# Moving the first loads of x and of the weights into one DMA queue, two weight chunks to a load, and dropping a touch load, at the head of a gated attention and FFN kernel

## The chip, the cores and the metric

The kernel runs on one core of a Trainium2 chip. The metric is the device time of one execution in microseconds (us). The kernel before takes 274.06 us (median of three runs, 273.92 to 274.57). A run counts as slow when it is over 1.5% above the fastest of the same kernel, and as fast otherwise; all runs that are compared here are fast unless the text says otherwise. In every profiled run the device time is 1.25 to 1.34 us longer than the span of the profile (for example 273.55 us against a span of 272.2 us).

Times of events are us from the start of the profile's span. "Landing" of a load means the last of its completion events in the DMA records of the trace.

## The reference, cut to what matters

```python
x = A_x                                            # (1, 2048, 640) bf16
g = sigmoid((x * gate_w).sum(-1))
q, k, v = split(x @ wqkv)                          # wqkv (640, 1920): columns q, k, v
a = linear_attention(phi(q), phi(k), v) @ wo       # phi(t) = (t + 1 or exp(t)) + 1e-6
b = (gelu(x @ w_gate) * (x @ w_up)) @ w_down
out = g * a + (1 - g) * b
```

The kernel computes the k and q projections first, for 16 tiles of 128 rows of x. Only this start matters here. It needs the first two tiles of x (x0, x1), the five 128-row chunks of the k columns of wqkv (wk0 to wk4) and the five of the q columns (wq0 to wq4). Each of these twelve blocks is 128 rows of 1280 bytes, 160 KB.

## The kernel before: the parts that the change and the argument touch

Loads are issued by SyncE ("sp") and by ScalarE ("act"); each has a DMA queue of its own. A load increments a semaphore, and its consumers wait for that.

```python
P.op("act", lambda e: e.dma_start(touch[0:16, 0:4], A_wqkv[0:128:8, 640:644]),   # 16 pieces of 8 B
     writes=[P.res("touch")], dma=new_dma_key())
load_x(0)
load_wk(0)
load_x(1, "act")
load_wk(1)
load_wk(3)
# ... a dummy Exp on ScalarE, so that its table is loaded early
load_wk(2, "act")
load_wk(4, "act")
P.op("dve", lambda e: e.memset(gw_sb, 0.0), writes=[r_gw])
dma_in(gw_sb[0:5, :], gate_w.rearrange("(k p) -> k p", p=128), [r_gw], eng="act")
for k in range(KC):                                # KC = 5
    load_wq(k, ("sp", "act")[k % 2])
# tiles 2..15 of x come transposed by DMA; the first of them waits for wk4
for i in range(NXN, NT):
    load_xT(i, after=([r_wk[4]] if i == NXN else ()))
```

TensorE's program at the head. `warm(n, w)` is n throw-away matmuls of w columns, which keep TensorE busy while it waits. `T` transposes a tile of x on TensorE, and VectorE copies the result back to SBUF. `KM(n, [k])` and `QM(n, [k])` are the projection of tile n by weight chunk k, each one matmul of 512 columns and one of 128 or 129.

```python
warm(5, 512)
warm(1, 128)
T(0, [0], 7)
T(0, [1, 2, 3, 4], 6)
warm(6, 128)
KM(0, [0])                  # needs wk0
T(1, [0], 7)                # needs x1
T(1, [1, 2, 3, 4], 6)
warm(3, 128)
KM(1, [0])
for k in (1, 2, 3):
    KM(0, [k])              # needs wk k
    KM(1, [k])
gate_col()                  # needs the gate weights
# ... chunk 4, then the ten QM of both tiles with the exp and max work between
for i in range(2, NT):
    KQ(i)                   # the tile loop: k and q projection of the other 14 tiles
```

## Time and profile before

| What | Value | Where it stands |
|---|---|---|
| device time | 274.06 us, median of 3 | times |
| TensorE busy | 267.9 of 272.2 us (98%) | busy table of the page |
| first projection matmul | 4.38 us | timeline |
| second weight chunk starts (KM of chunk 1) | 5.46 us | timeline |
| tile loop starts | 10.39 us | timeline |

TensorE is nearly always busy, but part of that at the head is throw-away work. So the question for a change of the first loads is at what time the useful chain starts, not how busy an engine is.

The chain of waits of the kernel before, its first pieces; columns are start (us), length (us), what. "SPq" is SyncE issuing a DMA, "PE ps" a matmul, L451 the 512-column matmul of KM.

```profile
0.79 0.41 SPq L340
...
1.26 2.98 DMA pool<-in_A_wqkv_dram
...
4.38 0.38 PE ps L451
```

The load that starts at 1.26 us is wk0. It takes 2.98 us to land, and the first projection matmul starts right after it. From there the chain stays on TensorE until 10.30 us.

TensorE's timeline of the kernel before; columns are start, length, engine, line, operation, output and input, count, and in brackets the idle time before and what ended it. L417 is warm-up, L431 the transposes, L451 and L452 are KM, L536 is the tile loop.

```profile
3.02 0.74 PE L431 MATMUL ps<-pool 128*128 128x128 bf16 x5
3.55 0.62 PE L417 MATMUL ps<-const-bfloat16-1.0 128*128 128x128 bf16 x6
4.38 0.38 PE L451 MATMUL ps<-pool 128*128 128x512 bf16 x1 [0.21 <-DMA pool<-in_A_wqkv_dram]
...
4.64 0.44 PE L431 MATMUL ps<-pool 128*128 128x128 bf16 x5
...
5.46 0.38 PE L451 MATMUL ps<-pool 128*128 128x512 bf16 x1
...
10.39 1.24 PE L536 MATMUL ps<-pool 128*128 128x512 bf16 x5
```

Tile 0 meets wk0 at 4.38, tile 1 is transposed at 4.64 when x1 has come, chunk 1 starts at 5.46, the tile loop at 10.39.

The DMA view of the kernel before, over 0 to 8 us in slices of 0.2 us: GB/s moved in each slice.

```profile
GB/s 0 0 0 0 0 0 0 0 0 186 179 282 269 147 83 243 365 384 301 275 275 371 378 378 397 384 391 353 245 259 270 275 359 390 410 365 403 391 339 254
```

The first slice with traffic is 1.8 to 2.0 us. The rate dips at 2.6 to 3.0 us (147 and 83 GB/s), is back at 365 at 3.2, and stays mostly above 270.

### The profile page before, as it was taken

To read this page: it belongs to the slowest core of one execution; us is meant where nothing else is said; L and a number is where in the kernel's file an instruction comes from. 1 tells how busy PE (TensorE), PEld (TensorE's weight loads), DVE (VectorE), ACT (ScalarE), POOL (GpSimd) and SP (SyncE) were. 2 spreads that over 40 slices of the span, in tenths; PEclk is the share of its full clock that TensorE was granted. 3 is DMA by queue.
4 is the path that set the end of the run, shared out by engine and by line. 5 is a ranking of instruction groups with operands and counts; after the bars stand their busy time and mean duration, and the time that the engine had idled before them with its cause. 6 is when DMAs were issued, how large, how long until landed. Compare 5 with 4: busy or idle time off the path is not lost.

```text
span 272.2 us, 3426 instructions
## 1 busy us (share of the span) xinstructions
PE 267.9 (98%) x1343; PEld 128.1 (47%) x1369; DVE 141.8 (52%) x251; ACT 75.9 (28%) x132; POOL 30.0 (11%) x28
## 2 busy tenths in 40 slices
PE   8999999999999999999999999999999999999997
PEld 4555555544445444444444444444444444444444
DVE  2689898997333335999999999634110000000200
ACT  2555555210422453332222232224011122121021
POOL 5000000003140002242332421000000000000000
PEclk9999999999999999999999999999999999999999
DMA  6776999500300011612221221272031110110211
GB/s 219 176 114 124 349 402 384 119 2 19 61 16 2 23 50 51 200 28 48 27 48 30 43 50 25 60 229 96 5 79 37 41 39 19 39 41 19 58 58 41
DMA packets 42208, 23.61 MB, mean 87 GB/s; under 512 B 31567, under 2 KB 40783, under 8 KB 42063
## 3 DMA queue, kind: packets, MB, share of 16 engines
q1 hardware_dynamic: 41429, 22.56, 30.5%
q10 hardware_dynamic: 762, 0.82, 0.8%
q8 instruction: 11, 0.18, 0.3%
q14 instruction: 6, 0.05, 0.1%
HBM read 13.83 MB, written 2.63 MB: 60 GB/s over the span
## 4 chain that ended last, share of the span: by engine, by line
PE 95%; DVE 2%; DMA 1%; issue 1%; ACT 1%; SPq 0%; DVEq 0%; ACTq 0%
PE ps L697 41%; PE ps L861 23%; PE ps L536 12%; PE ps L593 6%; PE ps L840 4%; PE ps L808 2%; PE ps L675 2%; PE ps L596 2%; DMA pool<-in_A_wqkv_dram 1%; PE ps L451 1%; PE ps L821 1%; PE ps L466 1%; DVE pool L490 1%; PE ps L718 1%; DVE pool L555 1%
## 5 line engine op out<-in xcount | busy, mean ns | idle before, releaser
L697 PE MATMUL ps<-pool 128*128 128x512 bf16 x510 | 113.0, 379 | 0.5
L697 PEld LDWEIGHTS ps<-pool 128*128 128x128 bf16 x520 | 50.4, 98 | 60.1
L861 PE MATMUL ps<-pool 128*128 128x512 bf16 (+2 forms) x300 | 62.4, 367 | 0.3
L703 ACT ACTIVATE pool<-ps 128x512 f32<-128x512 f32 x52 | 31.0, 597 | 73.1 <-PE ps L697 73.1
L705 DVE TENSOR_TENSOR pool<-ps,pool 128x512 bf16<-128x512 f32 x52 | 34.6, 689 | 31.7 <-PE ps L697 30.4
L861 PEld LDWEIGHTS ps<-pool 128*128 128x128 bf16 x306 | 29.1, 98 | 33.5 <-issue 0.4
L536 PE MATMUL ps<-pool 128*128 128x512 bf16 (+1 forms) x206 | 37.9, 344 | 0.2
L844 DVE TENSOR_TENSOR pool<-ps,pool 128x512 bf16<-128x512 f32 x4 | 2.8, 692 | 61.5 <-PE ps L840 61.5
L751 POOL TENSOR_TENSOR pool<-pool 128x640 f32<-128x640 bf16 x16 | 22.5, 1406 | 72.8 <-DVE pool L753 65.9
L868 ACT ACTIVATE pool<-ps,pool 128x512 bf16<-128x512 f32 (+1 forms) x16 | 10.9, 680 | 68.6 <-PE ps L861 68.6
L536 PEld LDWEIGHTS ps<-pool 128*128 128x128 bf16 x210 | 20.5, 98 | 17.5
L555 DVE SCALAR_TENSOR_TENSOR pool<-ps,pool 128x128 bf16<-128x128 f32 (+2 forms) x42 | 25.3, 603 | 2.4
L546 ACT ACTIVATE pool<-ps 128x640 bf16<-128x640 f32 x28 | 19.7, 703 | 18.1 <-DVE pool L555 10.6
L593 PE MATMUL ps<-pool 128*128 128x512 bf16 x76 | 19.2, 380 | 0.1
L761 DVE TENSOR_TENSOR pool<-pool 128x640 bf16<-128x640 bf16 x16 | 13.2, 825 | 0.6
L759 DVE TENSOR_SCALAR pool<-pool 128x32 f32<-128x32 f32 x16 | 12.8, 803 | 0.6
L753 DVE TENSOR_REDUCE pool<-pool 128x32 f32<-128x640 f32 x16 | 12.9, 809 | 0.0
L641 DVE TENSOR_TENSOR pool<-pool 128x640 f32<-128x640 f32 x14 | 11.6, 826 | 0.5
L840 PE MATMUL ps<-pool 128*128 128x512 bf16 x51 | 11.5, 380 | 0.1
L643 POOL PARTITION_ALL_REDUCE pool<-pool x1 | 4.0, 3971 | 60.7 <-DVE pool L641 60.7
L593 PEld LDWEIGHTS ps<-pool 128*128 128x128 bf16 x78 | 6.9, 98 | 7.2
L552 DVE TENSOR_SCALAR pool<-pool 128x640 bf16<-128x640 bf16 x28 | 9.1, 327 | 1.8 <-ACT pool L546 0.4
(70 smaller groups left out, 105.0 us busy)
## 6 DMA issues: line engine op xcount, KB each, us to landing
out_dram<-pool SPq DMA_DIRECT2D x19, 128.0 KB, 1.7
pool<-in_B_w_gate_dram SPq DMA_DIRECT2D x1, 2080.0 KB, 14.2
pool<-in_B_w_up_dram SPq DMA_DIRECT2D x1, 2080.0 KB, 18.8
pool<-in_A_x_dram SPq DMA_DIRECT2D x1, 1280.0 KB, 8.7
pool<-in_B_w_down_dram SPq DMA_DIRECT2D x1, 1120.0 KB, 6.1
pool<-omg_row SPq DMA_DIRECT2D x1, 1024.0 KB, 4.8
pool<-in_A_wqkv_dram SPq DMA_DIRECT2D x6, 160.0 KB, 4.4
pool<-in_A_x_dram SPq DMA_DIRECT2D x1, 960.0 KB, 5.8
```

Of the source, the lines that this page charges most:

```text
L536: last = e.matmul(ps[:, b + p, 0:c1 - c0], xT[:, k, i * 128:(i + 1) * 128], wkq[:, k, c0:c1], start=(k == 0), stop=(k == KC - 1))
L546: P.op("act", lambda e: e.activation(e_buf[m], ps_flat[:, o:o + 640], ACT.Exp), reads=banks, writes=[r_e[m]])
L555: P.op("dve", lambda e, c0=c0, c1=c1: e.scalar_tensor_tensor(dst[:, c0:c1], ps_flat[:, o + c0:o + c1], 1.0 + EPS, e_buf[m][:, c0:c1], ALU. ...
L593: last = e.matmul(ps[:, b, :], pk[i][:, c * 128:(c + 1) * 128], x_aug[:, i, 0:512], start=(i == 0), stop=(i == NT - 1))
L697: last = e.matmul(ps[:, b, :], w[:, k, fc * 128:(fc + 1) * 128], xT[:, k, j * 512:(j + 1) * 512], start=(k == 0), stop=(k == KC - 1))
L703: P.op("act", lambda e: e.activation(ge[n], ps[:, gb, :], ACT.Gelu_apprx_tanh), reads=[bank[gb]], writes=[r_ge[n]])
L705: P.op("dve", lambda e: e.tensor_tensor(hT[fc][:, j * 512:(j + 1) * 512], ps[:, ub, :], ge[n], ALU.mult), reads=[bank[ub], r_ge[n]], write ...
L751: P.op("pool", lambda e: e.tensor_tensor(tmp[n], pq[i], z_b, ALU.mult), reads=[r_pq[i], r_zb], writes=[r_tmp[n]])
L753: P.op("dve", lambda e: e.tensor_reduce(den[n], tmp[n].rearrange("p (h d) -> p h d", h=32), AX.X, ALU.add), reads=[r_tmp[n]], writes=[r_de ...
L761: P.op("dve", lambda e: e.tensor_tensor(pq[i].rearrange("p (h d) -> p h d", h=32), pq[i].rearrange("p (h d) -> p h d", h=32), den[n].unsqu ...
L840: last = e.matmul(ps[:, b, :], wd[:, fc, 512:640], hT[fc][:, j * 512:(j + 1) * 512], start=False, stop=(fc == NFC - 2), skip_group_check=True)
L861: last = e.matmul(ps[:, pb, 0:c1 - c0], lhs, rhs, start=False, stop=(q == len(rows) - 1), skip_group_check=True)
```

## The change

The intent is to give wk0, which gates the first projection, the DMA engines to itself: everything goes into SyncE's queue in the order of use, so nothing from a second queue runs beside wk0. The weights come mostly two chunks to a load, to save issues. The touch load goes, the gate weights are loaded first on ScalarE. The wait for wk4 before the transposed loads goes as well, since those now stand behind the weights in the same queue. Five warm-ups go, as less waiting is expected.

```diff
-            P.op("act", lambda e: e.dma_start(touch[0:16, 0:4], A_wqkv[0:128:8, 640:644]),
-                 writes=[P.res("touch")], dma=new_dma_key())
+            P.op("dve", lambda e: e.memset(gw_sb, 0.0), writes=[r_gw])
+            dma_in(gw_sb[0:5, :], gate_w.rearrange("(k p) -> k p", p=128), [r_gw], eng="act")
             load_x(0)
-            load_wk(0)
-            load_x(1, "act")
-            load_wk(1)
-            load_wk(3)
+            load_w(wk, 640, 0, 1, r_wk)
+            load_x(1)
+            load_w(wk, 640, 1, 3, r_wk)
+            load_w(wk, 640, 3, 5, r_wk)
+            load_w(wq, 0, 0, 2, r_wq)
+            load_w(wq, 0, 2, 4, r_wq)
+            load_w(wq, 0, 4, 5, r_wq)
 ...
-            load_wk(2, "act")
-            load_wk(4, "act")
-            P.op("dve", lambda e: e.memset(gw_sb, 0.0), writes=[r_gw])
-            dma_in(gw_sb[0:5, :], gate_w.rearrange("(k p) -> k p", p=128), [r_gw], eng="act")
-            for k in range(KC):
-                load_wq(k, ("sp", "act")[k % 2])
 ...
-                load_xT(i, after=([r_wk[4]] if i == NXN else ()))
+                load_xT(i)
 ...
             T(0, [1, 2, 3, 4], 6)
-            warm(6, 128)
+            warm(2, 128)
             KM(0, [0])
 ...
-            warm(3, 128)
+            warm(2, 128)
             KM(1, [0])
```

More of the change, by code (lines that the diff above doesn't have):

```diff
@@ L219, in bass_gated_mix__linear_attn_block__geglu_ffn__prompt_kernel @@
     O_GW = take(128)
-    O_TOUCH = take(16)
     TOTAL = off
@@ L300, in bass_gated_mix__linear_attn_block__geglu_ffn__prompt_kernel @@
             gw_sb = v16(O_GW, 128)
-            touch = v16(O_TOUCH, 16)
             bank = [P.res("bank%d" % b, excl=True) for b in range(8)]
@@ L341, in dma_in @@
                      reads=reads, writes=writes, dma=new_dma_key())
-            def load_x(i, eng="sp"):
-                dma_in(x_aug[:, i, 0:640], A_x[0, i * 128:(i + 1) * 128, :], [r_xn[i]], eng=eng)
-            def load_wk(k, eng="sp"):
-                dma_in(wk[:, k, :], A_wqkv[k * 128:(k + 1) * 128, 640:1280], [r_wk[k]], eng=eng)
-            def load_wq(k, eng="sp"):
-                dma_in(wq[:, k, 0:640], A_wqkv[k * 128:(k + 1) * 128, 0:640], [r_wq[k]], eng=eng)
-            P.op("act", lambda e: e.dma_start(touch[0:16, 0:4], A_wqkv[0:128:8, 640:644]),
-                 writes=[P.res("touch")], dma=new_dma_key())
@@ L357, in bass_gated_mix__linear_attn_block__geglu_ffn__prompt_kernel, with load_x, load_w @@
-            load_x(0)
-            load_wk(0)
-            load_x(1, "act")
-            load_wk(1)
-            load_wk(3)
+            def load_x(i):
+                dma_in(x_aug[:, i, 0:640], A_x[0, i * 128:(i + 1) * 128, :], [r_xn[i]])
+            def load_w(dst, c0, k0, k1, res):
+                dma_in(dst[:, k0:k1, 0:640],
+                       A_wqkv[k0 * 128:k1 * 128, c0:c0 + 640].rearrange("(k p) w -> p k w", p=128), res[k0:k1])
+            P.op("dve", lambda e: e.memset(gw_sb, 0.0), writes=[r_gw])
@@ L366, in bass_gated_mix__linear_attn_block__geglu_ffn__prompt_kernel, with load_xT @@
-            load_wk(4, "act")
-            P.op("dve", lambda e: e.memset(gw_sb, 0.0), writes=[r_gw])
-            dma_in(gw_sb[0:5, :], gate_w.rearrange("(k p) -> k p", p=128), [r_gw], eng="act")
-            for k in range(KC):
-                load_wq(k, ("sp", "act")[k % 2])
-            def load_xT(i, after=()):
+            def load_xT(i):
                 P.op("sp", lambda e: e.dma_start_transpose(xT[:, :, i * 128:(i + 1) * 128],
                                                            A_x[0, i * 128:(i + 1) * 128, :]),
-                     reads=list(after), writes=[r_xT[i]], dma=new_dma_key())
+                     writes=[r_xT[i]], dma=new_dma_key())
```

## The prediction

> **What bounds the kernel now.** TensorE: busy 267.9 of 272.2 us (98%, busy table), 95% of the chain of waits, granted clock full from 3.77 us on. Only the head can gain. There TensorE runs throw-away warm-ups until x0 lands (timeline); the chain of waits is SyncE's issue of x0 (at 0.79 us), the load of wk 0 (issued 1.26, 2.98 us long), then matmuls without a break to 10.23. So wk 0 gates the first projection matmul (4.38 us). Landings, from the DMA records: x0 2.97, wk0 4.24, x1 4.42, wk1 5.41, wk2 5.60, wk3 6.25, wk4 6.50, wq0 7.40, wq1 7.84, wq2 8.26, wq3 8.93, wq4 8.97, first transposed x tile (xT2) 10.19; its matmuls start at 10.39. After 4.38 TensorE waits for DMA only 0.16 us more (wk1).
>
> **What the change does.**
> 1. wk0 no longer shares the 16 engines with x1 and wk1. The Trainium skill (DMA: Bandwidth & Descriptors, "Queues, rings and completion order") says that an engine alternates between its rings packet by packet; the trace agrees: packets of both queues run side by side from 3.0 to 8.4 us. In one queue, wk0 follows x0 directly. 160 KB at the 326 to 360 GB/s of 4 to 8 us (windows table) is 0.46 to 0.50 us; estimated landings: wk0 3.5, x1 4.0, wk1-2 5.0, wk3-4 5.95, wq0-1 6.95, wq2-3 7.9, wq4 8.4.
> 2. Two chunks to a load delay the first of each pair by about 0.48 us, but TensorE takes a chunk each 0.55 us (5.46, 6.01, 6.55 in the timeline), so pairs stay ahead if the rate holds. SyncE issues a load each 0.47 us: eight end at 4.5, not limiting.
> 3. Five fewer warm-ups of 128 columns (0.06 us each at full clock, 0.11 at half): they only filled waiting. If wk0 lands at 3.5, the first projection matmul starts near 3.65, partly at half clock.
> 4. Touch load gone, gate weights earlier: x0 unchanged within 0.1 us.
> 5. The transposed loads no longer wait for wk4 (SyncE waited 2.5 us): issued from about 4.6 instead of 6.51, but behind the weights in the same queue, so xT2 lands 9.4 to 10.1, again only just before its use.
>
> **How much is on the critical path.** First projection matmul 0.7 us earlier; then x1 (4.0) and wk1-2 (5.0) stretch the gaps, so the second chunk starts at about 5.05 instead of 5.46: 0.4 us. From there TensorE is continuous, and the tile loop starts at about 10.0 instead of 10.39. Everything later is bound by TensorE, so the shift survives to the end.
>
> **Predicted time:** 273.7 us (0.13% less), range 273.1 to 274.3. Chances: faster by over 2% 0.003, within 2% 0.994, slower by over 2% 0.003. Any gain at all: about 85%.
>
> **What would show it.** wk0 landing at 3.4 to 3.7; first 128x512 projection matmul before 3.9; a short TensorE wait for wk1-2; tile loop starting at 9.9 to 10.2; later stages unchanged.
>
> **What would make it wrong.** A single queue that can't fill the engines (wk1-2 after 5.4); a slow first DMA without the touch load; the transposes taking engine time from wq; xT2 later than 10.2. The clock: the skill (TensorE: Matmul & The Clock Gate, "The HAM clock gate") says that activity over a window of about 3.4 us sets it; here it rose 2.95 us after the first warm-up, and fewer warm-ups with waits between could delay it, at up to about 0.5 us.

## The result, and the profile after

The changed kernel takes 274.06 us (median of six runs, 273.89 to 275.58), the kernel before 274.04 us in the same rounds (six runs, 273.85 to 274.57). The ratio is 1.0008, with a 95% interval of 0.9985 to 1.0032. A ratio here is the mean time of one kernel's fast runs over that of the other's of the same rounds, so not quite the ratio of the medians quoted. The time is the same; the forecast gain of 0.36 us isn't there.

The chain of waits of the changed kernel, its first pieces (L443 is now the 512-column matmul of KM):

```profile
0.79 0.40 SPq L338
...
1.25 0.41 SPq L338
...
1.70 0.43 SPq L338
...
2.18 3.84 DMA pool<-in_A_wqkv_dram
...
6.06 0.39 PE ps L443
```

The load in the chain is no longer wk0 but the pair wk1-2, issued at 2.18 us and landing 3.84 us later.

TensorE's timeline of the changed kernel (L409 warm-up, L423 transposes, L443 and L444 KM, L528 the tile loop):

```profile
3.19 0.63 PE L423 MATMUL ps<-pool 128*128 128x128 bf16 x5
3.65 0.28 PE L409 MATMUL ps<-const-bfloat16-1.0 128*128 128x128 bf16 x2
3.79 0.39 PE L443 MATMUL ps<-pool 128*128 128x512 bf16 x1
...
4.95 0.45 PE L423 MATMUL ps<-pool 128*128 128x128 bf16 x5 [0.71 <-DMA pool<-in_A_x_dram]
...
5.50 0.39 PE L443 MATMUL ps<-pool 128*128 128x512 bf16 x1
...
6.06 0.39 PE L443 MATMUL ps<-pool 128*128 128x512 bf16 x1
...
10.99 0.59 PE L528 MATMUL ps<-pool 128*128 128x512 bf16 x2
```

The first projection matmul does start 0.59 us earlier (3.79 against 4.38), as forecast. Then TensorE waits for x1 until 4.95, and for wk1-2 until 6.06. Without the second wait chunk 1 would have followed at about 5.77 (the matmul of 5.50 plus 0.27 us, the distance from 5.18 to 5.46 in the kernel before; an estimate). Chunk 1 starts 0.60 us later than before (6.06 against 5.46), and so does the tile loop (10.99 against 10.39). From chunk 1 to the loop both kernels take 4.93 us.

The DMA view of the changed kernel, again slices of 0.2 us over 0 to 8 us, GB/s:

```profile
GB/s 0 0 0 0 0 0 0 0 0 109 102 333 281 360 390 218 224 160 51 122 179 205 275 365 378 327 333 352 378 397 391 397 397 358 327 294 294 358 403 378
```

The one queue is fast at 2.2 to 3.0 us, when wk0 comes (390 GB/s). Then there is a dip at 3.0 to 4.4 us, down to 51 GB/s, longer than the one of before. It falls on x1 and wk1-2.

| Landing, us | before | before, second trace | after, forecast | after | after, second trace |
|---|---|---|---|---|---|
| x0 | 2.97 | 2.99 | 2.97 | 3.14 | 3.09 |
| wk0 | 4.24 | 4.34 | 3.5 | 3.50 | 3.48 |
| x1 | 4.41 | 4.51 | 4.0 | 4.91 | 5.06 |
| wk1 | 5.41 | 5.37 | 5.0 (pair 1-2) | 6.01 | 5.95 |
| wk2 | 5.60 | 5.55 | 5.0 | 6.01 | 5.95 |
| wq4 | 8.96 | 9.01 | 8.4 | 9.14 | 9.72 |
| tile loop starts | 10.39 | 10.56 | 10.0 | 10.99 | 11.16 |

The second traces are of the repetitions below (e1, e2).

**The head explains the span.** In all 14 traces the span minus the start of the tile loop is 261.74 to 261.82 us (272.21 - 10.39 = 261.82 before, 272.74 - 10.99 = 261.75 after). So everything behind the head is a constant, and the start of the tile loop is the measure for the experiments. It is not a measure of the first landings alone. From chunk 1 to the loop it is 4.92 to 4.95 us in six traces (before, e2, after, e3, e4, e12). It is longer in e1, e5, e6, e9 and e10 (5.08 to 7.73), where TensorE waits for later loads, and in e7, e8 and e11 (6.60, 5.20, 6.25), where it runs part of that stretch at half clock.

**Two cautions.** Both profiled runs of the kernel before (273.55 and 273.63 us) are quick ones for it: its 55 timed runs have a median of 274.06 us and lie between 273.27 and 276.87. So the 0.6 us between the traces overstate the difference: the timed runs have the changed kernel 0.02 to 0.27 us later (medians), with intervals that include zero. Only four of the 55 runs are as quick as 273.63 us. From the median of 274.06 us, the 1.25 to 1.34 us beside the span and the 261.82 us behind the loop's start, a typical run of the kernel before starts its loop at about 10.9 us (an estimate), close to the changed kernel's 10.99; no trace shows what holds it there. What the experiments can show is therefore where a gain is lost at the head, not a slowdown.

### The profile page after: what moved, and what is told of

It reads as the page before. It is cut to its first block, busy times and chain, and to the rows that moved or that the text cites. A ratio compares the mean times of both kernels' runs of the same rounds, so it can differ in the third digit from the quotient of the medians.

```text
span 272.7 us, 3437 instructions
## 1 busy us (share of the span) xinstructions
PE 269.2 (99%) x1364; PEld 127.9 (47%) x1364; DVE 142.0 (52%) x251; ACT 76.0 (28%) x132; POOL 30.0 (11%) x28
## 4 chain that ended last, share of the span: by engine, by line
PE 97%; DMA 1%; SPq 0%; DVE 0%; issue 0%
PE ps L689 41%; PE ps L853 23%; PE ps L528 14%; PE ps L585 6%; PE ps L832 4%; PE ps L800 2%; PE ps L667 2%; PE ps L588 1%; DMA pool<-in_A_wqkv_dram 1%; PE ps L458 1%; PE ps L813 1%; PE ps L443 1%; PE ps L710 1%; PE ps L728 0%; SPq L338 0%; PE ps L459 0%
## 5 line engine op out<-in xcount | busy, mean ns | idle before, releaser
L528 PE MATMUL ps<-pool 128*128 128x512 bf16 (+1 forms) x210 | 38.1, 344 | 0.0
L860 ACT ACTIVATE pool<-ps,pool 128x512 bf16<-128x512 f32 (+1 forms) x16 | 10.9, 681 | 68.6 <-PE ps L853 68.6
L528 PEld LDWEIGHTS ps<-pool 128*128 128x128 bf16 x210 | 20.5, 98 | 17.5
L538 ACT ACTIVATE pool<-ps 128x640 bf16<-128x640 f32 x28 | 19.7, 704 | 17.9 <-DVE pool L547 10.9
```

The source lines that it names most:

```text
L528: last = e.matmul(ps[:, b + p, 0:c1 - c0], xT[:, k, i * 128:(i + 1) * 128], wkq[:, k, c0:c1], start=(k == 0), stop=(k == KC - 1))
L538: P.op("act", lambda e: e.activation(e_buf[m], ps_flat[:, o:o + 640], ACT.Exp), reads=banks, writes=[r_e[m]])
```

## The experiments

Beside landings I count how many of the twelve 160 KB blocks are over by 5.0 us: the packets of 1280 bytes that had ended by then in the DMA records, divided by 128. I call it the front at 5.0 us. It is 5.36 and 5.49 in the two traces of the kernel before, and 4.45 and 4.69 in those of the changed kernel.

The theories at the outset: (A) chance of one execution; (C) the missing touch load; (D) GpSimd's mask building writes to SBUF at the same time. Later ones: small packets, pairing, one queue against two, order.

### e1 and e2: each kernel again

No edit.

> The changed kernel again, unedited. Theory A (chance of the single execution: the stretch of slow DMA packets that held x1 to 4.90 us comes and goes from run to run): in this profile x1 lands before 4.3 and the tile loop starts at 10.0 to 10.5 or the stretch sits at another load. Theory B (systematic in this load order): x1 again lands at 4.7 to 5.1, wk1-2 at 5.8 to 6.2, and the tile loop starts at 10.9 to 11.1. Time within 0.15% of before under both.

> The kernel before again, unedited, timed against itself: ratio 1.000 with an interval that shows the noise. The first trace had 273.55 us, below the 274.04 median, with the tile loop starting at 10.39. If that trace was a lucky one, this trace starts its loop at about 10.9 (median minus 273.55 is 0.5 us); if it was typical, at 10.3 to 10.5.

e1: x1 landed at 5.06 us, wk1-2 at 5.95, the loop started at 11.16. The time was 274.24 us (five runs) against 273.97 us (eleven), ratio 1.0012, interval 0.9998 to 1.0026. e2: the loop started at 10.56 us, time 273.98 us, ratio 1.0004 (0.9989 to 1.0019).

The lines of e1's timeline:

```profile
3.85 0.63 PE L443 MATMUL ps<-pool 128*128 128x512 bf16 x1
...
5.11 0.72 PE L423 MATMUL ps<-pool 128*128 128x128 bf16 x5 [0.51 <-DMA pool<-in_A_x_dram]
...
6.08 0.38 PE L443 MATMUL ps<-pool 128*128 128x512 bf16 x1
```

Theory A falls: the late x1 and wk1-2 come back in the second trace, in the same place. Here chunk 1 at 6.08 follows the matmul of 5.81 without a gap, so it was x1 that held it; the pair, landing at 5.95, would have held it to nearly the same time. e2 was between its two expectations for the loop; the profile of the kernel before is reproducible, but its timed median of 273.98 us is 0.35 us above this profiled run.

### e3: the touch load put back

```diff
+            P.op("act", lambda e: e.dma_start(touch[0:16, 0:4], A_wqkv[0:128:8, 640:644]),
+                 writes=[P.res("touch")], dma=new_dma_key())
             P.op("dve", lambda e: e.memset(gw_sb, 0.0), writes=[r_gw])
 ...
+            nc.sync.wait_ge(dma_sems[0], 16)
             nc.sync.wait_ge(s_out, n_out)
```

> The changed kernel with the touch load put back at the head of ScalarE's queue (and a wait for it at the end). Theory C (the touch load took the cold latency away): x0 lands at 2.97 as before instead of 3.15, x1 at about 4.0, wk1-2 at about 5.0, tile loop at about 10.0 to 10.2, time 0.3 to 0.9 us less than the changed kernel. If the touch load doesn't matter: x0 at 3.1 to 3.2, the rest like the changed kernel's.

x0 landed at 3.02 us, but x1 at 4.96 and wk1-2 at 6.30; front 4.43, loop at 11.28, time 274.41 us, ratio 1.0029 (1.0005 to 1.0053). Theory C falls. The touch load may be worth some 0.1 us for x0, but e4 and e5 have x0 at 3.01 and 3.05 without it, so even that isn't shown.

### e4: the mask built later

```diff
-                P.op("pool", lambda e: e.memset(mask, 1.0), writes=[r_mask])
+                P.op("pool", lambda e: e.memset(mask, 1.0), reads=[r_pk[2]], writes=[r_mask])
```

> The changed kernel with GpSimd's mask building (2.2 to 4.7 us, 128x600 and 128x40 selects) held back until pk tile 2 is written. Theory D (GpSimd's writes to SBUF slow the DMA writes of that stretch): the slow packets between 3.0 and 4.5 go, x1 lands at about 4.0 and wk1-2 at 5.0, time 0.4 to 0.9 us less than the changed kernel. If GpSimd has no part: the slow stretch stays, x1 at 4.7 to 5.1.

GpSimd was idle between 2 and 5 us, as meant. x1 landed at 4.08 us, but wk1-2 only at 6.32; front 4.75, loop at 11.31, time 274.47 us, ratio 1.0020 (1.0004 to 1.0036). The slow stretch moved by a load and stayed. Theory D falls.

### e5: the gate weights later

```diff
-            dma_in(gw_sb[0:5, :], gate_w.rearrange("(k p) -> k p", p=128), [r_gw], eng="act")
 ...
             load_w(wk, 640, 3, 5, r_wk)
+            dma_in(gw_sb[0:5, :], gate_w.rearrange("(k p) -> k p", p=128), [r_gw])
             load_w(wq, 0, 0, 2, r_wq)
```

> The changed kernel with the gate weights' load (five packets of 256 B, at 2.3 to 2.6 us) moved from ScalarE's queue to SyncE's, after wk3-4. Small-packet theory (a few tiny packets set off the slow stretch that follows them; in both traces of the kernel before, slow packets also began at 5.4 to 5.6, with the gate packets): no slow stretch from 3.0 to 4.5, x1 lands at about 4.0, 5.3 or more loads are over by 5.0 us, the tile loop starts at 10.0 to 10.4. Against it: x1 again at 4.7 to 5.1, 4.4 to 4.7 loads over by 5.0, the loop at 10.9 to 11.3.

x1 landed at 5.08 us, front 4.71, loop at 11.56 (after 0.49 us of waiting for the first pair of wq, until 8.84), time 274.55 us, ratio 1.0011 (0.9997 to 1.0026). The stretch is there without any small packet near it, so small packets aren't what sets it off. There were slow packets again at 5.8 to 6.9 us, beside the gate packets, which also is when the wq loads begin; the run can't separate these two.

### e6: one queue, one chunk to a load

```diff
-            load_w(wk, 640, 1, 3, r_wk)
-            load_w(wk, 640, 3, 5, r_wk)
-            load_w(wq, 0, 0, 2, r_wq)
-            load_w(wq, 0, 2, 4, r_wq)
-            load_w(wq, 0, 4, 5, r_wq)
+            for k in range(1, KC):
+                load_w(wk, 640, k, k + 1, r_wk)
+            for k in range(KC):
+                load_w(wq, 0, k, k + 1, r_wq)
```

> All loads in SyncE's queue as in the change, but one chunk to each load. Pairing theory: the slow stretch stays (4.4 to 4.8 loads over by 5.0 us), but wk1 lands about 0.3 to 0.45 us before the pair did, so the tile loop starts 0.2 to 0.45 us earlier than the changed kernel's (10.99 and 11.16): 10.6 to 10.9. If pairing costs nothing: 10.9 to 11.2. If two chunks to a load themselves made the slow stretch: 5.3 loads over by 5.0 and the loop at 10.0 to 10.4.

wk1 landed at 5.29 us instead of 6.01 and 5.95, so waiting for a pair does cost the first chunk up to 0.7 us (0.10 to 0.25 us of it is x1's own earlier landing). But the front is 4.68, x1 came at 4.81, and the later blocks came slower than in pairs: wk4 at 7.57, wq4 at 10.24 (against 9.14 and 9.72). TensorE then waited for wk and wq chunks, and the loop started at 11.06, like the changed kernel's. The time is 274.14 us, ratio 0.9996 (0.9982 to 1.0009). So pairs aren't the cause of the slow stretch. They cost the first chunk; that they pay it back later is what these single traces suggest, not more. The gain I had expected from singles didn't come.

### e7: two queues, pairs kept

```diff
             load_x(0)
+            load_x(1, "act")
             load_w(wk, 640, 0, 1, r_wk)
-            load_x(1)
             load_w(wk, 640, 1, 3, r_wk)
-            load_w(wk, 640, 3, 5, r_wk)
+            load_w(wk, 640, 3, 5, r_wk, "act")
             load_w(wq, 0, 0, 2, r_wq)
-            load_w(wq, 0, 2, 4, r_wq)
+            dma_in(gw_sb[0:5, :], gate_w.rearrange("(k p) -> k p", p=128), [r_gw], eng="act")
+            load_w(wq, 0, 2, 4, r_wq, "act")
             load_w(wq, 0, 4, 5, r_wq)
```

(the gate load at the head goes, as it stands here.)

> Pairs kept, queues split again (x0, wk0, wk1-2, wq0-1, wq4 on SyncE; x1, wk3-4, gate weights, wq2-3 on ScalarE; no touch load). Two-queue theory (with two rings an engine goes on with the other ring's packet while one packet is slow): 5.2 or more loads over by 5.0 us as in the kernel before, x1 by 4.6, the tile loop at 10.4 to 10.8. If the number of queues doesn't matter: 4.4 to 4.8 loads over by 5.0, loop at 10.9 or later.

The front at 5.0 us was 5.89, the best of all, and x1 landed at 3.91. The DMA view of e7, same slices:

```profile
GB/s 0 0 0 0 0 0 0 0 0 134 96 166 250 352 397 378 365 352 371 403 384 362 323 307 294 262 250 166 96 186 173 230 301 339 358 371 384 397 347 364
```

There is no dip at 3.0 to 4.4 us, but one at 5.2 to 6.2 (96 GB/s), and it falls on wk1-2, which landed at 8.66 us, after wk3-4 (13 of its 16 completion events had come by 5.96). TensorE sat idle for 2.5 us before its matmul (list of waits), its granted clock fell to a half at 9.18 us and rose again at 12.60, and the loop started at 15.31. Two of the six runs are slow, and the times of the others spread from 274.35 to 278.40 us, so the ratio of 1.0063 (1.0016 to 1.0111) says only that this isn't better. For the theory: two queues had the front that was expected, but the dip was moved, not removed.

### e8: x1 alone on ScalarE's queue

```diff
             load_x(0)
+            load_x(1, "act")
+            dma_in(gw_sb[0:5, :], gate_w.rearrange("(k p) -> k p", p=128), [r_gw], eng="act")
             load_w(wk, 640, 0, 1, r_wk)
-            load_x(1)
             load_w(wk, 640, 1, 3, r_wk)
```

(the gate load at the head goes here too.)

> The changed kernel with x1 alone moved to ScalarE's queue, ahead of the gate weights. Two-queue theory: x1 lands by 4.5, wk1-2 at 5.4 to 5.6, the tile loop starts at 10.4 to 10.7, time 0.2 to 0.5 us less than the changed kernel. If x1 is slow whatever its queue: x1 at 4.7 to 5.1, loop at 10.9 to 11.2.

The front was 5.31, as in the kernel before, and x1 landed at 3.74 us. But x0, now beside x1, landed at 3.54 instead of 3.1, wk0 at 4.04, and the pair wk1-2 at 5.82. The loop started at 11.32 us, time 274.24 us, ratio 1.0010 (0.9984 to 1.0036). Part of the expectation held (x1, the front), part failed (wk1-2, the loop). An earlier x1 was paid for by x0. TensorE's timeline:

```profile
4.30 0.63 PE L443 MATMUL ps<-pool 128*128 128x512 bf16 x1
...
5.58 0.63 PE L443 MATMUL ps<-pool 128*128 128x512 bf16 x1
...
6.12 0.63 PE L443 MATMUL ps<-pool 128*128 128x512 bf16 x1
```

The pair had landed when chunk 1 started at 6.12, straight behind the matmuls of chunk 0, so TensorE did not wait for it. What held the loop was the late x0 and then the clock: three matmuls of 512 columns took 0.63 us each, as in the stretch of e7 whose granted clock is a half, against 0.38 in the kernel before. (e8 has no clock record of its own.) So this loop start says little about the loads.

### e9 and e10: each load cut in halves over the two queues

```diff
+            def halves(dst, src, res):
+                key = new_dma_key()
+                P.op("act", lambda e: e.dma_start(dst[64:128], src[64:128]), writes=[P.res("half")], dma=key)
+                P.op("sp", lambda e: e.dma_start(dst[0:64], src[0:64]), writes=res, dma=key)
```

`load_x` and `load_w` call it, the gate load comes after wk3-4; e10 also loads wk1 and wk2 singly.

> The load order and the pairs of the change, but each load is cut in two by rows: rows 0 to 63 in SyncE's queue, rows 64 to 127 in ScalarE's; gate weights on ScalarE after wk3-4. Two-queue theory: the front holds (5.2 or more loads over by 5.0 us, against 4.4 to 4.8 in every single-queue trace), x1 lands by 4.4, wk1-2 by 5.5, the tile loop starts at 10.2 to 10.6. Order theory (the strict order x0, wk0, x1, wk1-2 itself meets slow packets): 4.4 to 4.8 loads over by 5.0, x1 at 4.7 to 5.1, loop at 10.9 to 11.3.

> The same with wk1 and wk2 as loads of their own. Two-queue theory with pairing cost: wk1 lands 0.3 to 0.45 us before the pair of e9 did, at about 4.9 to 5.1, and the tile loop starts at 10.0 to 10.4, time 0.2 to 0.5 us less than the kernel before. Order theory: as for e9, 4.4 to 4.8 loads over by 5.0, loop at 10.8 or later.

Both missed, on the slow side of every expectation: fronts 3.68 and 3.99, loops at 13.33 and 13.68, times 276.63 us (four runs) and 276.85 us (six), ratios 1.0093 (1.0077 to 1.0110) and 1.0113 (1.0088 to 1.0138). The timeline of e9 shows a cost that I hadn't counted; columns as before, ACTq and SPq are the issues of DMAs:

```profile
0.79 0.56 SPq L346 DMA_DIRECT2D pool<-in_A_x_dram  x1
1.39 0.87 ACTq L345 DMA_DIRECT2D pool<-in_A_wqkv_dram  x1
1.41 0.58 SPq L346 DMA_DIRECT2D pool<-in_A_wqkv_dram  x1
2.03 0.60 SPq L346 DMA_DIRECT2D pool<-in_A_x_dram  x1
```

A half costs 0.56 to 0.60 us to issue on SyncE, more than a whole block in the kernel before (0.41 to 0.43 us), and a block takes one issue on each queue: SyncE's pitch of 0.62 us is longer than the 0.47 us in which a block moves at 350 GB/s. The test was therefore confounded by its own issue cost and says nothing about one queue against two. It does agree with the Trainium skill (DMA: Bandwidth & Descriptors, "Rules for kernel authors"), which advises against cutting a transfer into partition halves and for one transfer of 128 partitions; here the kernel with the cut took 2.7 us more than the kernel before (276.63 against 273.96 us, medians).

### e11: x1 before wk0, one queue

```diff
-            load_w(wk, 640, 0, 1, r_wk)
             load_x(1)
+            load_w(wk, 640, 0, 1, r_wk)
             load_w(wk, 640, 1, 3, r_wk)
```

> The changed kernel, one queue, with x1 before wk0. Two-queue theory: the front is as slow as in any single queue, 4.4 to 4.8 loads over by 5.0 us, and whatever stands third and fourth (wk0, wk1-2) is late: wk0 at 4.6 to 5.1, loop at 10.9 or later. Order theory (x1 read beside or right after x0 is quick, x1 after wk0 is slow): x1 lands by 3.6, wk0 by 4.2, 5.2 or more loads over by 5.0, loop at 10.3 to 10.7.

x1 landed at 3.60 us, but wk0, now third, at 4.88, and wk1-2 at 6.72; front 4.65. As in the changed kernel the slow stretch hit what stood third (in e4 it hit the fourth), so it is neither x1 as such nor the order x1 behind wk0. The time is 274.51 us, ratio 1.0031 (1.0008 to 1.0055). The profiled run took 276.13 us, with the loop at 13.04: its granted clock rose only at 9.49 us, against 3.59 in the changed kernel's first trace. The other runs are at 274.21 to 274.62, and one at 275.74.

### e12: everything of the change but the queues and the pairs

```diff
-            P.op("act", lambda e: e.dma_start(touch[0:16, 0:4], A_wqkv[0:128:8, 640:644]),
-                 writes=[P.res("touch")], dma=new_dma_key())
+            P.op("dve", lambda e: e.memset(gw_sb, 0.0), writes=[r_gw])
+            dma_in(gw_sb[0:5, :], gate_w.rearrange("(k p) -> k p", p=128), [r_gw], eng="act")
 ...
-            P.op("dve", lambda e: e.memset(gw_sb, 0.0), writes=[r_gw])
-            dma_in(gw_sb[0:5, :], gate_w.rearrange("(k p) -> k p", p=128), [r_gw], eng="act")
 ...
-            warm(6, 128)
+            warm(2, 128)
 ...
-            warm(3, 128)
+            warm(2, 128)
```

against the kernel before, so with its two queues, its single chunks and its wait for wk4.

> The kernel before, with its two queues and its single-chunk loads, but with the change's other parts: no touch load, the gate weights' load in its place at the head of ScalarE's queue, 2 and 2 warm-ups. If merging the queues is what cost the change its gain: 5.2 or more loads over by 5.0 us, the tile loop at 10.1 to 10.6, time at or up to 0.3 us below the kernel before (ratio 0.999 to 1.000); wk0 a little earlier (3.8 to 4.2), as x1 is issued some 0.3 us later. If the touch load or the warm-ups were what kept the kernel before quick: 4.8 or fewer loads over by 5.0, or the loop at 10.9 or later.

This was meant to confirm the two-queue theory, and it went against it. Its DMA view:

```profile
GB/s 0 0 0 0 0 0 0 0 0 147 134 323 297 321 352 186 51 38 192 250 288 314 275 307 352 403 333 384 371 378 352 314 307 301 346 390 365 391 403 333
```

With two queues full of single chunks the dip is at 3.0 to 3.6 us (51 and 38 GB/s), as in the changed kernel: front 4.54, wk0 at 4.27, x1 at 5.75, wk1 at 5.95, loop at 11.55. The time is 274.74 us against 274.06, ratio 1.0012 (0.9972 to 1.0051). If the chip doesn't matter, two queues are not enough to keep the front of the kernel before. But the run differs in more: it was made on another chip than e1 to e11 (9 instead of 0), where no trace of the kernel before was taken, and its chain of waits begins with the gate load's issue on ScalarE (1.01 to 1.57 us), which puts x1's issue at 1.60 instead of 1.23. It met its other expectation, which blamed the missing touch load or the warm-ups. e3 shows that the touch load doesn't help with one queue (front 4.43); with two queues it was not tried apart from the rest.

### What the 14 traces say together

| Trace | queues | blocks to a load | third whole block issued at | GB/s, 2.0 to 3.0 | GB/s, 3.5 to 5.0 | front at 5.0 | loop starts |
|---|---|---|---|---|---|---|---|
| before, e2 | two | 1 | 1.26 | 192, 195 | 342, 358 | 5.36, 5.49 | 10.39, 10.56 |
| e7 | two | 1 and 2 | 1.21 | 252 | 351 | 5.89 | 15.31 |
| e8 | x1 apart | 1 and 2 | 1.26 | 277 | 265 | 5.31 | 11.32 |
| after, e1 | one | 1 and 2 | 1.71 | 293, 295 | 218, 242 | 4.45, 4.69 | 10.99, 11.16 |
| e3, e4, e5 | one | 1 and 2 | 1.71 | 286, 288, 307 | 207, 217, 270 | 4.43, 4.75, 4.71 | 11.28, 11.31, 11.56 |
| e6 | one | 1 | 1.71 | 292 | 236 | 4.68 | 11.06 |
| e11 | one | 1 and 2 | 1.70 | 289 | 255 | 4.65 | 13.04 |
| e12 | two | 1 | 1.60 | 286 | 269 | 4.54 | 11.55 |
| e9, e10 | halves on both | 1 and 2 | 2.29 | 201, 187 | 196, 237 | 3.68, 3.99 | 13.33, 13.68 |

The two columns of GB/s are from the windows view. Every trace has a stretch of slow packets early in its traffic: packets of 1280 bytes that take 0.15 us or more, the longest of a trace 0.51 to 1.22 us, where the usual one takes 0.055 us (0.074 in e9). The time of all such packets above the usual, summed over 1.5 to 9.5 us and divided by the 16 engines, is 0.45 and 0.62 us in the two traces of the kernel before, and 0.69 and 0.74 in those of the changed one. In the kernel before the stretch comes at 2.4 to 3.2 us, right behind x0 (a smaller one follows at 5.4 to 6.2); in the kernels with one queue it comes at 3.0 to 4.5 us, behind two blocks that came quickly, and TensorE has then nothing to do. In these traces, that is where the expected gain went: wk0 came earlier, and the stretch fell on the next two loads instead.

What sets the stretch off is open. Chance, the touch load, the mask building, the gate packets, the pairs, the order of x1 and wk0 were each taken away, and it stayed; two queues alone don't avoid it (e12, with the reserves named there). Each variant has one trace. One thing fits the fronts of all 14 traces: where three whole blocks are issued by 1.3 us, the front at 5.0 us is 5.3 or more, and where the third is issued at 1.6 us or later, it is under 4.8. The rates from 3.5 to 5.0 us fit less well (e8). No run isolates this, and both traces of the kernel before are of quick runs, so it is an observation and not a cause.

## Why the prediction was right or wrong

**Right.** The class (within 2%) and the range (273.1 to 274.3 us, measured 274.06) held. This is owed to the width of the range and not to the mechanism: the range reaches above the 274.04 us of the kernel before, so it also covers no gain at all, and the gain, given a chance of about 85%, didn't come. "The shift survives to the end" held as a rule: in all 14 traces the part behind the start of the tile loop is 261.74 to 261.82 us. wk0 landing at 3.4 to 3.7 us: 3.50 and 3.48. First projection matmul before 3.9: 3.79. Issues of SyncE not limiting, transposes from about 4.6: they began at 4.70, and xT2 landed at 9.79 (forecast 9.4 to 10.1; 10.38 in the second trace), so TensorE didn't wait for it.

**Wrong: the step that failed.** The gain of 0.36 us failed in step 1, at "estimated landings: wk0 3.5, x1 4.0, wk1-2 5.0". The step took the rate of 4 to 8 us in the kernel before (326 to 360 GB/s) for the whole head. wk0 did come at that rate. Behind it, the windows view of the changed kernel has, for 2 to 3, 3 to 4 and 4 to 5 us (the last column is GB/s):

```profile
2.00:3.00 1.00, 1.00 (x4) 0.29 (x2) 0.00 (x0) 0.99 (x2) 0.93 (x2) 1.00 0.90 293
3.00:4.00 1.00, 1.00 (x10) 0.69 (x9) 0.37 (x2) 0.09 (x1) 0.93 (x2) 1.00 0.75 155
4.00:5.00 1.00, 0.29 (x3) 0.05 (x2) 0.28 (x1) 0.00 (x0) 0.58 (x3) 1.00 0.89 280
```

and the kernel before has:

```profile
2.00:3.00 1.00, 1.00 (x4) 0.29 (x2) 0.00 (x0) 0.99 (x1) 0.93 (x2) 1.00 0.83 192
3.00:4.00 1.00, 1.00 (x13) 0.98 (x11) 0.43 (x2) 0.20 (x1) 0.93 (x2) 1.00 0.96 314
4.00:5.00 1.00, 0.79 (x12) 0.54 (x10) 0.32 (x2) 0.00 (x0) 0.57 (x3) 1.00 1.00 360
```

The change won 101 GB/s for one us (293 - 192) and lost 159 and 80 in the next two. The sum is 138 KB less by 5.0 us, which is 0.4 us at 350 GB/s (an estimate from these lines). x1 landed at 4.91 instead of 4.0, wk1-2 at 6.01 instead of 5.0. The prediction put wk0's 2.98 us in the kernel before down to the shared engines and doesn't mention the dip there at 2.6 to 3.0 us; it left no room for such a dip in the one queue, where it stood at 3.0 to 4.4 us. It had named the sign, "wk1-2 after 5.4", but with the reason that a single queue can't fill the engines. The sign came; the reason doesn't fit, since the same queue moved 357 and 374 GB/s in the two us after 5.0 (342 and 307 in e1), where the kernel before moved 326 and 341 (289 and 347 in e2).

**Step 2, pairs.** "Pairs stay ahead if the rate holds" has its condition in it, and the rate did not hold. The delay of the first chunk of a pair measured 0.7 us (e6: wk1 at 5.29 us against 6.01 and 5.95 for the pair) against 0.48 forecast; counted from the landing of x1 it is 0.41 to 0.62, so the forecast held. After 6.06 us TensorE had no DMA wait in the first trace of the changed kernel, so behind the dip the pairs did stay ahead there; in the second it stopped for about 0.15 us before the first wq chunk, whose pair landed at 8.30.

**Step 4.** "x0 unchanged within 0.1 us" was a little off: 3.14 and 3.09 us against 2.97 and 2.99.

**The two citations.** The engines' alternation between rings fits wk0's earlier landing (3.50 against 4.24), but so does the dip, which in the kernel before stood in wk0's way and in the changed one came behind it; no run parts the two. The same page says, under "Issuing engines are not separate DMA queues", that issuing from several engines only saves issue time. Here e12 and e6, with single chunks on two queues and on one, have fronts of 4.54 and 4.68, which agrees; the 5.36 of the kernel before and e7's 5.89, both on two queues, leave it less simple. The clock didn't spoil the changed kernel: it rose at 3.59 us. The danger named in the prediction, that waits between warm-ups delay the rise (TensorE: Matmul & The Clock Gate, "The HAM clock gate"), came true in part: the rise was late in other runs with waits, at 9.49 us in e11's profiled run, which took 276.13 us, and at 5.03 in e5's, and e8's first three 512-column matmuls ran at half clock. No run parts the waits from chance here.

**No version found that beats both.** e6 at a ratio of 0.9996 is the best of ten variants, and that is no difference.

## What to carry to other kernels

When a change clears the way for the load that gates the start, look at the next two loads as well: here the chain moved from wk0 to wk1-2, and 0.59 us won at the first matmul had become 0.60 us lost at the second chunk. Ask whether the traces that you compare are of typical runs: both of the kernel before were quick ones. A rate read from a steady stretch isn't the rate of the first microseconds; use the slices of that stretch itself, and don't assume that a dip belongs to the thing that happens beside it. Check by one mark (here the start of the tile loop) whether all of the rest is a constant: if it is, traces of the head say more than timed runs whose spread is larger than the gain.

## What the Trainium skill lacked or had wrong

- DMA: Bandwidth & Descriptors, "Latency and other measured facts": it gives an average and a high-load figure for HBM access, and nothing on the start of a kernel. In every trace here, packets of 1280 bytes that usually take 0.055 us took 0.15 us or more, up to 0.51 to 1.22 us by trace, in a stretch within the first 4.5 us of traffic; in the four DMA views shown the rate fell to 83, 51, 96 and 38 GB/s in a slice of 0.2 us. No run shows whether HBM is the reason.
- The same page, "Issuing engines are not separate DMA queues": it calls the issue time usually small against the DMA. For the 160 KB loads here an issue took 0.35 to 0.47 us. That is small against the 2.2 to 4.4 us from issue to landing (medians of the kernel before), but not against the 0.47 us in which a block moves at 350 GB/s.
- The same page, "Rules for kernel authors": the advice against partition halves held, but it has no size. Here the halves took 0.56 to 0.60 us each to issue on SyncE, and the kernel took 2.7 us more than the kernel before (276.63 against 273.96 us).
- No page of it says how many loads should be under way before the first one lands. In the 14 traces, 5.3 or more blocks were over by 5.0 us where three whole blocks were issued by 1.3 us, and under 4.8 elsewhere; no run isolates this as the cause.
